# An expert layer behind polysketch attention on one core: the expert stage rewritten with 128-slot tiles

## Chip, core and metric

The kernel runs on one core of one Trainium2 chip. The metric is device time in microseconds (us) of one execution. All data is float32, except that S1 and S2 come as float64.

## What is computed

```python
def phi(x):                       # x: [batch 4, heads 4, seq 1088, 32]
    a = einsum('rd,bhsd->bhsr', S1, x); b = einsum('rd,bhsd->bhsr', S2, x)   # r = 8
    return einsum('bhsi,bhsj->bhsij', a, b).reshape(..., 64)
kv = einsum('bhsf,bhsd->bhfd', phi(k), v);  z = phi(k).sum(axis=2)
attn = (phi(q) @ kv) / (phi(q) . z + 1e-6)
x = attn as [4352 tokens, 128]
logits = x @ w_gate;  e_idx = argmax(logits)          # 8 experts, one per token
gate_w = softmax(logits)[e_idx];  eom = sigmoid(x @ w_output_gate)
out[n] = gate_w[n] * eom[n, e] * (relu(x[n] @ w1[e]) @ w2[e])    # w1: 128x1024, w2: 1024x128
```

With the inputs of the reference the eight experts get 547, 583, 461, 483, 494, 867, 420 and 497 tokens.

## The kernel before

The kernel has two stages.

**Attention and routing.** The 4352 tokens go in nine groups of up to 512. For each group `k_steps` builds the keys' features and adds up their products with the values in PSUM; `q_steps` builds the queries' features, the attention output `x` (`nd`, L310), the logits and the routing (`route`, L336 to L387). At the end of `route`, GpSimd (POOL) writes each token's row (128 values, the factor of its output and its token number) into the DRAM buffer `xs`, sorted by expert: one indirect DMA for 128 tokens (L385), 34 in all. Behind them POOL writes rows of padding behind each expert's last token (L431), so that each expert's rows fill whole tiles of `TS` slots. Meanwhile VectorE (DVE) turns the counts of tokens into two tables (L436 to L469): `eti`, the expert of each tile, and `bti`, the first row of each tile in `xs`. There is one tile for each of the `NT` steps that the program unrolls. `NT` is the most tiles that any routing could need, (4352 + 8·255) // 256 = 24; the tokens above fill 20, and the last four hold padding alone.

**Experts.** A tile is 256 slots. `fetch` (L476) lets SyncE (SP) read the tile's expert and first row from the tables into registers, and issues two DMAs: the expert's 1 MB of weights into one of three buffers (skipped where the buffer already holds this expert), and the tile's rows into `xin`. `up` (L485) turns the two 128-row halves of `xin` (two transposes on TensorE, L488), copies them to SBUF (DVE, L490) and multiplies them with w1: eight matmuls of 256 columns with the weights stationary (L495), in two PSUM tiles of four. ScalarE (ACT) takes the first tile through the relu (L497), DVE the second (L499). `down` (L502) multiplies with w2: eight matmuls with the weights stationary and the activations `hT` moving, summed in one PSUM tile (L506), whose result has the features on partitions, so that it is copied (ACT, L508), turned back by two transposes (L514), scaled by the token's factor (DVE, L517) and written to its tokens' rows of `out` by two indirect DMAs (POOL, L519). A float32 matmul appears in the trace as two MATMUL instructions, each with its own weight load (PEld), and a transpose as one.

Two things set the order of the work. Instructions are put on each engine by the scheduler of the framework, which may move them within the program's dependencies. And two writes to the same DRAM buffer are kept in order: an indirect DMA into `xs` or `out` waits until the one before it has landed.

```python
for t in range(min(NW, NT)):
    fetch(t)
up(0)
for t in range(NT):
    if t + 1 < NT:
        up(t + 1)
    yT = down(t)
    if t + NW < NT:
        fetch(t + NW)
    send(t, yT)
```

Of the kernel before, what the change touches and what calls it, by code (L numbers as in the profile page):

```python
# [29 lines left out]
def kernel(  # L30
# [61 lines left out]
    # Queries and keys with the features of two heads on partitions, twice, for the two parts of S1  # L92
    # and S2; values with tokens on partitions (two heads and a column of ones, twice).
# [47 lines left out]
    before = consts.tile([128, 128], F32, tag="before")     # [s, t]: s < t  # L141
# [16 lines left out]
    PP = 128 // E                       # partitions that pad one expert  # L158
    padsel = consts.tile([128, E], F32, tag="padsel")       # [p, e]: p // PP == e
# [18 lines left out]
    upto = consts.tile([128, E, E], F32, tag="upto")        # [e, f]: f <= e  # L178
# [4 lines left out]
    def split():  # L183
        # A float64 as two float32: the upper 23 bits of its fraction, and the lower 29.
# [88 lines left out]
    seen = {"tile": None, "at": 0}  # L273

    def q_steps(g):
# [60 lines left out]
        def route():  # L336
# [47 lines left out]
            for j in range(nj):  # L384
                nc.gpsimd.indirect_dma_start(  # L385
                    out=xs[:, :], out_offset=bass.IndirectOffsetOnAxis(ap=sloti[:, j:j + 1], axis=0),
                    in_=s["x"][:, j], in_offset=None, bounds_check=E * CAP - 1)  # L387
# [13 lines left out]
    for g in range(len(groups) + 1):  # L401
# [29 lines left out]
    nc.gpsimd.indirect_dma_start(  # L431
        out=xs[:, :], out_offset=bass.IndirectOffsetOnAxis(ap=pai[:, :1], axis=0),
        in_=pad.rearrange("p a b -> p (a b)"), in_offset=None)
# [28 lines left out]
    # A tile behind the last one falls on the padding of the last expert.  # L462
# [21 lines left out]

    def up(t):  # L485
        ps = ps_t("ps_xs")[:, :TS]
        for i in range(NI):
            nc.tensor.transpose(ps[:, i * 128:(i + 1) * 128], xin[t][:, i, :DM], ident)  # L488
# [3 lines left out]
        for g in range(FC // 4):  # L492
            ps = ps_w("ps_h").rearrange("p a (c x) -> p (a c) x", x=TS)
            for c in range(4):
                nc.tensor.matmul(ps[:, c], wt[t % NW][:, 0, 4 * g + c], xT, start=True, stop=True)  # L495
            if g % 2 == 0:
                nc.scalar.activation(hT[:, 4 * g:4 * g + 4], ps, ACTF.Relu)  # L497
            else:
                nc.vector.tensor_scalar_max(hT[:, 4 * g:4 * g + 4], ps, 0.0)  # L499
# [69 lines left out]
```

## Time and profile before

| | |
|---|---|
| time, median of three runs | 380.53 us (379.42 to 381.73) |
| span of the profiled execution | 381.2 us |
| PE busy | 302.9 us, 79% |
| weight loads (PEld) busy | 248.8 us, 65% |
| DVE, ACT, POOL busy | 117.4, 54.7, 85.2 us |
| DMA, mean over the span | 108 GB/s |
| attention and routing, last DVE step of the tables ends | 145.8 us |
| first TensorE work of the experts | 173.2 us |
| last indirect DMA issued by POOL | 372.6 us |

The profiled execution's own time is its span of 381.2 us; no time outside the span is listed for it. The page names the engines PE (matmul), PEld (weight load), DVE, ACT, POOL and SP. A line such as L495 is a line of the kernel. In rows of the timeline the columns are: start, length, engine, line, operation, out<-in with shapes, count of instructions merged into the row, and in brackets how long the engine stood idle before it and what ended that.

### The profile page before, as it was taken

Reading aid. Unit: us, or ns where it says so; the run is one execution under the profiler, and the core shown is the slowest. Engines: PE = TensorE matmul, PEld = TensorE weight load, DVE = VectorE, ACT = ScalarE, POOL = GpSimd, SP = SyncE. Lnnn points to the kernel's source line nnn. Section 1 sums busy time; section 2 is a strip of 40 time slices with the busy share of each in tenths; the row PEclk is TensorE's granted clock in tenths of the full one; section 3 lists DMA queues with packets and bytes.
Section 4 is the critical chain, followed back from the end, with each engine's and each line's share of the span. In section 5 each row is a group of like instructions: output and inputs, shape, how many; then the busy total and the mean of one; then the engine's idle time right before and its main releaser. Section 6 shows DMA issues by size and latency. Waiting matters only on the chain. (4 is left out here: it accounts for less than half of the span.)

```text
span 381.2 us, 4504 instructions
## 1 busy us (share of the span) xinstructions
PE 302.9 (79%) x1501; PEld 248.8 (65%) x1501; DVE 117.4 (31%) x413; ACT 54.7 (14%) x94; POOL 85.2 (22%) x115
## 2 busy tenths in 40 slices
PE   2979899999997530007999988999999999999950
PEld 2976677778755420006888777778778888788840
DVE  5211265635564452001222222223222232322300
ACT  1001122202221100001211111121111211112100
POOL 4000004322433333300112212322223222233231
PEclk9999899968999655556999999999999999999995
DMA  6999900000000004117345455444543544410000
GB/s 160 259 250 245 241 23 21 23 21 22 24 28 24 21 29 128 59 71 263 94 156 152 138 167 164 170 152 138 158 140 91 204 146 138 135 49 20 2 0 0
DMA packets 18870, 41.21 MB, mean 108 GB/s; under 512 B 3146, under 2 KB 9932, under 8 KB 16160
## 3 DMA queue, kind: packets, MB, share of 16 engines
q1 hardware_dynamic: 16080, 35.36, 32.4%
q0 software_dynamic: 2768, 5.57, 4.3%
q8 instruction: 12, 0.20, 0.2%
q14 instruction: 10, 0.08, 0.1%
HBM read 39.55 MB, written 6.47 MB: 121 GB/s over the span
## 5 line engine op out<-in xcount | busy, mean ns | idle before, releaser
L506 PE MATMUL ps_y<-hT,wt 128*128 128x256 f32 x384 | 90.6, 379 | 0.0
L495 PE MATMUL ps_h<-xsT,wt 128*128 128x256 f32 x384 | 89.0, 385 | 0.5 <-DVE xsT L490 0.5
L519 POOL DMA_INDIRECT out_dram<-y,xin x48 | 46.7, 972 | 166.2 <-DVE y L517 56.8
L495 PEld LDWEIGHTS ps_h<-xsT,wt 128*128 128x128 f32 x384 | 73.5, 193 | 12.4 <-DVE xsT L490 2.2
L506 PEld LDWEIGHTS ps_y<-hT,wt 128*128 128x128 f32 x384 | 71.1, 190 | 8.7
L385 POOL DMA_INDIRECT xs<-x,sloti x34 | 33.4, 983 | 119.4 <-DVE sloti L375 56.2
L499 DVE TENSOR_SCALAR hT<-ps_h 128x1024 f32<-128x1024 f32 x24 | 29.4, 1225 | 86.8 <-PE ps_h L495 69.1
L497 ACT ACTIVATE hT<-ps_h 128x1024 f32<-128x1024 f32 x24 | 24.6, 1024 | 105.6 <-PE ps_h L495 105.6
L488 PE MATMUL ps_xs<-ident,xin 128*128 128x128 f32 x48 | 9.9, 288 | 36.9 <-DMA xin<-xs 36.8
L490 DVE COPY xsT<-ps_xs 128x256 f32<-128x256 f32 x24 | 10.2, 424 | 75.9 <-PE ps_xs L488 75.9
L488 PEld LDWEIGHTS ps_xs<-ident,xin 128*128 128x128 f32 x48 | 6.1, 143 | 41.5 <-DMA xin<-xs 40.0
L265 PEld LDWEIGHTS ps_kvz<-vt,kp 128*128 128x128 f32 (+1 forms) x144 | 24.4, 255 | 8.1 <-DVE kp L244 4.1
L265 PE MATMUL ps_kvz<-vt,kp 128*128 128x65 f32 (+1 forms) x144 | 25.2, 341 | 3.8 <-DVE kp L244 3.2
L283 PE MATMUL ps_fa<-qT,Sa 128*128 128x512 f32 (+1 forms) x36 | 21.5, 714 | 1.3 <-DVE qp L295 1.3
L238 PEld LDWEIGHTS ps_ab<-S12blk,kT 128*128 128x128 f32 x136 | 20.8, 241 | 1.6 <-DVE S12blk L220 1.1
L238 PE MATMUL ps_ab<-S12blk,kT 128*128 128x32 f32 x136 | 20.9, 316 | 1.0 <-DMA kT<-in_k_dram 1.0
L508 ACT COPY yT<-ps_y 128x256 f32<-128x256 f32 x24 | 8.9, 373 | 88.5 <-PE ps_y L506 88.5
L303 PE MATMUL ps_nd<-kz,qp 128*128 128x66 f32 (+1 forms) x144 | 18.5, 279 | 1.0 <-ACT a_sb L290 1.0
L303 PEld LDWEIGHTS ps_nd<-kz,qp 128*128 128x128 f32 (+1 forms) x144 | 17.1, 191 | 3.0 <-ACT a_sb L290 1.4
L283 PE MATMUL ps_fb<-qT,Sb 128*128 128x512 f32 (+1 forms) x36 | 18.2, 633 | 0.0
L244 DVE TENSOR_TENSOR kp<-ps_ab,b_sb 128x1024 f32<-128x1024 f32 (+1 forms) x9 | 10.5, 1165 | 20.5 <-ACT b_sb L241 20.5
L295 DVE TENSOR_TENSOR qp<-a_sb,ps_fb 128x1024 f32<-128x1024 f32 (+1 forms) x9 | 10.4, 1161 | 14.8 <-PE ps_fb L283 14.8
(120 smaller groups left out, 179.1 us busy)
## 6 DMA issues: line engine op xcount, KB each, us to landing
wt<-in_w_dram SPq DMA_DIRECT2D x24, 1024.0 KB
kT<-in_k_dram SPq DMA_DIRECT2D x16, 256.0 KB, 8.5
qT<-in_q_dram SPq DMA_DIRECT2D x16, 256.0 KB, 7.8
xin<-xs SPq DMA_DIRECT2D x24, 130.0 KB, 2.2
vt<-in_v_dram SPq DMA_DIRECT2D x8, 260.0 KB, 7.2
out_dram<-y,xin POOLq DMA_INDIRECT x48, 2.3
xs<-x,sloti POOLq DMA_INDIRECT x34, 2.3
kT<-in_k_dram SPq DMA_DIRECT2D x2, 128.0 KB, 8.1
```

The costliest lines, as they stand in the source:

```text
L238: nc.tensor.matmul(ps[:, j * H + 2 * p:j * H + 2 * p + 2], kT[:, p, c * 128:(c + 1) * 128], S12blk, start=True, stop=True)
L244: nc.vector.tensor_mul(kp[:, :n], bview(av, [list(av.ap[1]), list(av.ap[2]), [0, r]]), bview(bv, [list(bv.ap[1]), [0, r], list(bv.ap[2])]))
L265: nc.tensor.matmul(acc[b][:, p], s["kp"][p0:p0 + np_, j * H + 2 * p:j * H + 2 * p + 2].rearrange("s h i j -> s (h i j)"), vt[p0:p0 + np_, ...
L283: nc.tensor.matmul(ps[:, p, :n], S_.rearrange("p h i j -> p (h i j)"), qT[:, p, cols(cs)], start=True, stop=True)
L303: nc.tensor.matmul(ps[p0:p0 + np_, p, j], s["qp"][:, p, j * 128 + p0:j * 128 + p0 + np_], kvz_done[b][:, p], start=True, stop=True)
L385: nc.gpsimd.indirect_dma_start(out=xs[:, :], out_offset=bass.IndirectOffsetOnAxis(ap=sloti[:, j:j + 1], axis=0), in_=s["x"][:, j], in_offs ...
L488: nc.tensor.transpose(ps[:, i * 128:(i + 1) * 128], xin[t][:, i, :DM], ident)
L495: nc.tensor.matmul(ps[:, c], wt[t % NW][:, 0, 4 * g + c], xT, start=True, stop=True)
L497: nc.scalar.activation(hT[:, 4 * g:4 * g + 4], ps, ACTF.Relu)
L499: nc.vector.tensor_scalar_max(hT[:, 4 * g:4 * g + 4], ps, 0.0)
L506: nc.tensor.matmul(ps, wt[t % NW][:, 1, c], hT[:, c], start=(c == 0), stop=(c == FC - 1))
L519: nc.gpsimd.indirect_dma_start(out=out, out_offset=bass.IndirectOffsetOnAxis(ap=x.bitcast(I32)[:, i, DM + 1:DM + 2], axis=0), in_=y[:, i], ...
```

## The change

The expert stage is written anew. A tile has 128 slots (`TS`), so `NT` becomes (4352 + 8·127) // 128 = 41; the tokens above fill 37. In `up` one transpose and eight matmuls of 128 columns remain, all into one two-bank PSUM tile, of which ACT takes the first half through the relu and DVE the second. In `down` the activations `hT` are the stationary side and the weights w2 the moving one: the result has tokens on partitions, so the copy and the two transposes back go away, and ACT scales by the token's factor as it empties the PSUM tile (L512 of the new file). One indirect DMA writes the tile to `out`. The indirect DMAs into `xs`, and those into `out`, are declared independent of each other (`apart`). All three weight buffers are filled with expert 0's weights right behind the loads of keys and queries, and the weight load of the first three tiles is skipped where the expert is 0. `fetch` loads the rows ahead of the weights; there are five `xin` buffers for four. SP keeps the order in which the program is written (`manual_schedule`).

```diff
-TS = 256
+TS = 128
+    def apart(group, ins):
+        tc.declare_no_dep(ins.ins, group=group, reason="the rows are distinct")
+        tc.add_to_no_dep_group(group, ins.ins)
...
+    wt = [consts.tile([128, 2, FC, 128], F32, tag=f"wt{i}", name=f"wt{i}") for i in range(NW)]
+    for i in range(NW):
+        nc.sync.dma_start(wt[i].rearrange("p a c x -> p (a c x)"), w_d[0])
...
-                nc.gpsimd.indirect_dma_start(
+                apart("rows", nc.gpsimd.indirect_dma_start(
...
     def fetch(t):
+        at = nc.sync.value_load(bti[0:1, t:t + 1], min_val=0, max_val=E * CAP - TS)
+        xin[t] = work.tile([TS, W], F32, tag="xin", bufs=NW + 2, name="xin")
+        nc.sync.dma_start(xin[t], xs[bass.ds(at, TS), :])
         regs[t] = nc.sync.value_load(eti[0:1, t:t + 1], min_val=0, max_val=E - 1)
-        kw = {} if t < NW else {"cond": regs[t] != regs[t - NW]}
         nc.sync.dma_start(wt[t % NW].rearrange("p a c x -> p (a c x)"),
-                          w_d[bass.ds(regs[t], 1)].rearrange("e p x -> p (e x)"), **kw)
-        at = nc.sync.value_load(bti[0:1, t:t + 1], min_val=0, max_val=E * CAP - TS)
...
+                          w_d[bass.ds(regs[t], 1)].rearrange("e p x -> p (e x)"),
+                          cond=regs[t] != (regs[t - NW] if t >= NW else 0))
 
     def up(t):
...
+        nc.tensor.transpose(ps, xin[t][:, :DM], ident)
...
+        ps = ps_w("ps_h").rearrange("p a (c x) -> p (a c) x", x=TS)
+        for c in range(FC):
+            nc.tensor.matmul(ps[:, c], wt[t % NW][:, 0, c], xT, start=True, stop=True)
+        nc.scalar.activation(hT[:, :FC // 2], ps[:, :FC // 2], ACTF.Relu)
+        nc.vector.tensor_scalar_max(hT[:, FC // 2:], ps[:, FC // 2:], 0.0)
...
     def down(t):
-            nc.tensor.matmul(ps, wt[t % NW][:, 1, c], hT[:, c], start=(c == 0), stop=(c == FC - 1))
-        yT = work.tile([128, TS], F32, tag="yT", name="yT")
-        nc.scalar.copy(yT, ps)
...
+        ps = psum.tile([TS, DM], F32, tag=("kvz", "rt")[t % 2], name="ps_y")
+            nc.tensor.matmul(ps, hT[:, c], wt[t % NW][:, 1, c], start=(c == 0), stop=(c == FC - 1))
+        y = work.tile([TS, DM], F32, tag="y", bufs=4, name="y")
+        nc.scalar.activation(y, ps, ACTF.Copy, scale=x[:, DM:DM + 1])
+        apart("out", nc.gpsimd.indirect_dma_start(
...
+    with tc.manual_schedule(engines={mybir.EngineType.SP}):
+        for t in range(NW):
+            fetch(t)
+        up(0)
+        for t in range(NT):
+            if t + 1 < NT:
+                up(t + 1)
+            down(t)
+            if t + NW < NT:
+                fetch(t + NW)
```

**Where the built programs put it.** The listings below give one engine's instructions in program order; a row ends with the semaphores that the instruction waits for (named after the engine or DMA lane that raises them).

TensorE in the middle of the expert stage before: `ps_h` is the first matmul of the next tile, `ps_y` the second matmul of this one, `ps_xs` and `ps_yt` the transposes.

```order
L506 MATMUL ps_y_1556<-hT_1482,wt0_1271 128x256
L495 MATMUL ps_h_1544<-xsT_1541,wt1_1272 128x256 [waits DMAHW0_49,DVE_49]
L495 MATMUL ps_h_1544<-xsT_1541,wt1_1272 128x256 x3
L495 MATMUL ps_h_1550<-xsT_1541,wt1_1272 128x256 [waits PE_49]
L495 MATMUL ps_h_1550<-xsT_1541,wt1_1272 128x256 x3
L506 MATMUL ps_y_1556<-hT_1482,wt0_1271 128x256 x7
L488 MATMUL ps_xs_1599<-ident_121,xin_1525 128x128 [waits DMAHW3_49]
```

And the same place in the changed program, one whole tile and the start of the next:

```order
L501 MATMUL ps_h_1465<-xsT_1462,wt0_121 128x128 [waits DMAHW2_49,PE_49]
L501 MATMUL ps_h_1465<-xsT_1462,wt0_121 128x128 x7
L495 MATMUL ps_xs_1511<-ident_127,xin_1448 128x128 [waits DMAHW3_49]
L510 MATMUL ps_y_1527<-wt0_121,hT_1464 128x128 [waits Activation_49]
L510 MATMUL ps_y_1527<-wt0_121,hT_1464 128x128 x3
L510 MATMUL ps_y_1527<-wt0_121,hT_1464 128x128 [waits DVE_49]
L510 MATMUL ps_y_1527<-wt0_121,hT_1464 128x128 x3
L501 MATMUL ps_h_1516<-xsT_1513,wt1_122 128x128 [waits DMAHW4_49,PE_49]
```

Before, the eight matmuls `ps_h` of the next tile stand between the first and the second `ps_y` of this one; now a tile's eight `ps_y` stand behind its own eight `ps_h` with one transpose between.

VectorE for the same tile of the changed program (`hT_1464` is written half by ACT, L502, and half by DVE, L503):

```order
L497 COPY xsT_1513<-ps_xs_1511 128x128 [waits DVE_49,PE_49]
L503 TENSOR_SCALAR hT_1464<-ps_h_1465 128x512 [waits Activation_49]
L497 COPY xsT_1564<-ps_xs_1562 128x128 [waits DVE_49,PE_49]
L503 TENSOR_SCALAR hT_1515<-ps_h_1516 128x512 [waits Activation_49]
```

and ScalarE:

```order
L512 ACTIVATE y_1485<-ps_y_1476,xin_1330 128x128 [waits DMAHW7_49,PE_49]
L502 ACTIVATE hT_1464<-ps_h_1465 128x512 [waits DVE_49,PE_49]
L512 ACTIVATE y_1536<-ps_y_1527,xin_1397 128x128 [waits DMAHW1_49,PE_49]
```

Before, each half of the relu read a PSUM tile of its own and waited for PE by itself; now both halves read one tile, and DVE's half names ACT's semaphore and no other.

SyncE at the start of the expert stage before (TENSOR_LOAD reads a table entry into a register):

```order
L477 TENSOR_LOAD eti [waits DVE_49]
L477 ISA x2
L479 ISA
L479 DMA wt_1271<-in_w_dram 128x2048 [waits DMAHW0_49]
L481 TENSOR_LOAD bti [waits DVE_49]
L481 ISA x2
L477 TENSOR_LOAD eti
```

There 42 TENSOR_LOADs stand in all between this first weight DMA and the first `xin` DMA. In the changed program:

```order
L485 TENSOR_LOAD bti [waits DVE_49]
L485 ISA x2
L487 ISA
L487 DMA xin<-xs 128x130 [waits DMAHW3_49,DMASW2_49]
L488 TENSOR_LOAD eti
L488 ISA x2
L489 REGISTER_ALU x2
L489 ISA
L489 DMA wt_121<-in_w_dram 128x2048 [waits DMAHW4_49,DMAHW0_49]
```

Now one TENSOR_LOAD stands ahead of the first `xin` DMA, and each tile's two reads stand with its two DMAs.

## Rows read from the trace of the kernel before

**Rows 1.** Windows: busy us of each engine (instructions), then PEclk, DMA share, GB/s.

```profile
300.00:350.00 50.00, 47.91 (x230) 40.74 (x229) 13.28 (x20) 8.75 (x13) 12.39 (x13) 1.00 0.36 118
```

**Rows 2.** Waits over the whole span: total us, times, longest us.

```profile
POOL xs L385 <- DMA xs<-x,sloti: 52.7, 28, 3.3
PEld ps_xs L488 <- DMA xin<-xs: 40.0, 10, 32.4
```

**Rows 3.** Timeline, 140 to 175 us: from the routing to the experts.

```profile
142.31 0.16 DVE L381 TENSOR_TENSOR x<-co,ex 128x2 f32<-128x2 f32 x1
...
143.68 0.17 DVE L461 CAST eti<-et 128x24 int32<-128x24 f32 x1
...
144.02 0.35 DVE L464 TENSOR_TENSOR tu<-tu,num 128x192 f32<-128x192 f32 x1
...
144.89 0.37 SPq L479 DMA_DIRECT2D wt<-in_w_dram  x1
...
145.58 0.18 DVE L469 CAST bti<-bt 128x24 int32<-128x24 f32 x1
...
156.58 0.97 POOL L385 DMA_INDIRECT xs<-x,sloti  x1 [1.64 <-DMA xs<-x,sloti]
159.70 0.96 POOL L431 DMA_INDIRECT xs<-pad,pai  x1 [2.15 <-DMA xs<-x,sloti]
170.93 0.41 SPq L483 DMA_DIRECT2D xin<-xs  x1
...
173.17 0.69 PE L488 MATMUL ps_xs<-ident,xin 128*128 128x128 f32 x2 [32.35 <-DMA xin<-xs]
...
174.37 5.27 PE L495 MATMUL ps_h<-xsT,wt 128*128 128x256 f32 x16 [0.52 <-DVE xsT L490]
```

**Rows 4.** DMA issues: count and median us from issue to landing.

```profile
xs<-x,sloti POOLq DMA_INDIRECT x34, 2.3
...
xs<-pad,pai POOLq DMA_INDIRECT x1, 4.9
```

**Rows 5.** Timeline, 298 to 318 us: a weight load, and one tile of the experts.

```profile
300.41 0.35 SPq L479 DMA_DIRECT2D wt<-in_w_dram  x1
...
301.61 3.62 PE L495 MATMUL ps_h<-xsT,wt 128*128 128x256 f32 x16
...
305.06 3.19 PE L506 MATMUL ps_y<-hT,wt 128*128 128x256 f32 x14
...
308.33 0.37 ACT L508 COPY yT<-ps_y 128x256 f32<-128x256 f32 x1 [3.73 <-PE ps_y L506]
...
308.76 0.44 PE L514 MATMUL ps_yt<-ident,yT 128*128 128x128 f32 x2 [0.30 <-ACT yT L508]
...
309.47 3.62 PE L495 MATMUL ps_h<-xsT,wt 128*128 128x256 f32 x16
```

**Rows 6.** Timeline of PE, 60 to 100 us: matmuls of few columns.

```profile
70.70 1.87 PE L238 MATMUL ps_ab<-S12blk,kT 128*128 128x32 f32 x16
72.41 1.04 PE L323 MATMUL ps_l<-wg,xT 128*128 128x16 f32 x8
```

**Rows 7.** Timeline, 100 to 141 us: ACT and DVE over 512 columns of PSUM.

```profile
120.61 0.59 ACT L320 COPY xT<-ps_xt 128x512 f32<-128x512 f32 x1 [2.53 <-PE ps_xt L318]
...
121.55 0.69 DVE L295 TENSOR_TENSOR qp<-a_sb,ps_fb 128x512 f32<-128x512 f32 x1 [0.91 <-PE ps_fb L283]
```

**Rows 8.** Windows of 1 us: PE busy (instructions), PEclk, DMA share, GB/s.

```profile
117.00:118.00 1.00, 0.10 (x1) 1.00 0.00 0
...
177.00:178.00 1.00, 1.00 (x5) 0.73 0.99 418
...
304.00:305.00 1.00, 1.00 (x6) 1.00 0.96 349
305.00:306.00 1.00, 1.00 (x7) 1.00 0.27 80
```

**Rows 9.** Timeline, 352 to 382 us: the end.

```profile
367.80 0.37 ACT L508 COPY yT<-ps_y 128x256 f32<-128x256 f32 x1 [4.04 <-PE ps_y L506]
...
372.59 0.97 POOL L519 DMA_INDIRECT out_dram<-y,xin  x1 [1.43 <-DMA out_dram<-y,xin]
```

More of the change, by code (lines that the diff above doesn't have):

```diff
@@ L384, in route @@
             for j in range(nj):
-                nc.gpsimd.indirect_dma_start(
+                apart("rows", nc.gpsimd.indirect_dma_start(
                     out=xs[:, :], out_offset=bass.IndirectOffsetOnAxis(ap=sloti[:, j:j + 1], axis=0),
-                    in_=s["x"][:, j], in_offset=None, bounds_check=E * CAP - 1)
+                    in_=s["x"][:, j], in_offset=None, bounds_check=E * CAP - 1))
         return fa, fb, nd, logits, route
@@ L430 @@
     nc.vector.tensor_copy(pai, pa)
-    nc.gpsimd.indirect_dma_start(
+    apart("rows", nc.gpsimd.indirect_dma_start(
         out=xs[:, :], out_offset=bass.IndirectOffsetOnAxis(ap=pai[:, :1], axis=0),
-        in_=pad.rearrange("p a b -> p (a b)"), in_offset=None)
+        in_=pad.rearrange("p a b -> p (a b)"), in_offset=None))
     tk = consts.tile([128, E, KN], F32, tag="tk")
@@ L469 @@
     nc.vector.tensor_copy(bti, bt)
-    wt = [consts.tile([128, 2, FC, 128], F32, tag=f"wt{i}", name=f"wt{i}") for i in range(NW)]
-    NI = TS // 128
     regs, xin, hTs = {}, {}, {}
     def fetch(t):
+        at = nc.sync.value_load(bti[0:1, t:t + 1], min_val=0, max_val=E * CAP - TS)
+        xin[t] = work.tile([TS, W], F32, tag="xin", bufs=NW + 2, name="xin")
+        nc.sync.dma_start(xin[t], xs[bass.ds(at, TS), :])
         regs[t] = nc.sync.value_load(eti[0:1, t:t + 1], min_val=0, max_val=E - 1)
-        kw = {} if t < NW else {"cond": regs[t] != regs[t - NW]}
         nc.sync.dma_start(wt[t % NW].rearrange("p a c x -> p (a c x)"),
-                          w_d[bass.ds(regs[t], 1)].rearrange("e p x -> p (e x)"), **kw)
-        at = nc.sync.value_load(bti[0:1, t:t + 1], min_val=0, max_val=E * CAP - TS)
-        xin[t] = work.tile([128, NI, W], F32, tag="xin", bufs=NW + 1, name="xin")
-        nc.sync.dma_start(xin[t], xs[bass.ds(at, TS), :].rearrange("(i p) w -> p i w", p=128))
+                          w_d[bass.ds(regs[t], 1)].rearrange("e p x -> p (e x)"),
+                          cond=regs[t] != (regs[t - NW] if t >= NW else 0))
     def up(t):
         ps = ps_t("ps_xs")[:, :TS]
-        for i in range(NI):
-            nc.tensor.transpose(ps[:, i * 128:(i + 1) * 128], xin[t][:, i, :DM], ident)
+        nc.tensor.transpose(ps, xin[t][:, :DM], ident)
         xT = work.tile([128, TS], F32, tag="xsT", name="xsT")
@@ L491, in up @@
         hT = work.tile([128, FC, TS], F32, tag="hT", name="hT")
[L492 to L499, printed above, removed]
+        ps = ps_w("ps_h").rearrange("p a (c x) -> p (a c) x", x=TS)
@@ L500, in up @@
+        for c in range(FC):
+            nc.tensor.matmul(ps[:, c], wt[t % NW][:, 0, c], xT, start=True, stop=True)
+        nc.scalar.activation(hT[:, :FC // 2], ps[:, :FC // 2], ACTF.Relu)
+        nc.vector.tensor_scalar_max(hT[:, FC // 2:], ps[:, FC // 2:], 0.0)
         hTs[t] = hT
     def down(t):
-        hT = hTs.pop(t)
-        ps = psum.tile([128, TS], F32, tag="kvz", name="ps_y")
+        hT, x = hTs.pop(t), xin.pop(t)
+        ps = psum.tile([TS, DM], F32, tag=("kvz", "rt")[t % 2], name="ps_y")
@@ L505, in down @@
         for c in range(FC):
-            nc.tensor.matmul(ps, wt[t % NW][:, 1, c], hT[:, c], start=(c == 0), stop=(c == FC - 1))
-        yT = work.tile([128, TS], F32, tag="yT", name="yT")
-        nc.scalar.copy(yT, ps)
-        return yT
-    def send(t, yT):
-        ps = psum.tile([128, NI, DM], F32, tag="rt", name="ps_yt")
-        for i in range(NI):
-            nc.tensor.transpose(ps[:, i], yT[:, i * 128:(i + 1) * 128], ident)
-        y = work.tile([128, NI, DM], F32, tag="y", bufs=3, name="y")
-        x = xin.pop(t)
-        nc.vector.tensor_tensor(y, ps, x[:, :, DM:DM + 1].to_broadcast((128, NI, DM)), op=ALU.mult)
-        for i in range(NI):
-            nc.gpsimd.indirect_dma_start(
-                out=out, out_offset=bass.IndirectOffsetOnAxis(ap=x.bitcast(I32)[:, i, DM + 1:DM + 2], axis=0),
-                in_=y[:, i], in_offset=None, bounds_check=N - 1, oob_is_err=False)
@@ L523 @@
-    for t in range(min(NW, NT)):
-        fetch(t)
-    up(0)
-    for t in range(NT):
-        if t + 1 < NT:
-            up(t + 1)
-        yT = down(t)
-        if t + NW < NT:
-            fetch(t + NW)
-        send(t, yT)
+            nc.tensor.matmul(ps, hT[:, c], wt[t % NW][:, 1, c], start=(c == 0), stop=(c == FC - 1))
+        y = work.tile([TS, DM], F32, tag="y", bufs=4, name="y")
+        nc.scalar.activation(y, ps, ACTF.Copy, scale=x[:, DM:DM + 1])
+        apart("out", nc.gpsimd.indirect_dma_start(
+            out=out, out_offset=bass.IndirectOffsetOnAxis(ap=x.bitcast(I32)[:, DM + 1:DM + 2], axis=0),
+            in_=y, in_offset=None, bounds_check=N - 1, oob_is_err=False))
```

## Prediction

> **What bounds the kernel now.** I read the windows first, then the waits, then the timeline at the places that they point to. The reader is to see two different limits.
>
> In the expert stage TensorE is the limit. In 300 to 350 us it is busy for 47.91 of 50 us at a granted clock of 1.00, with the DMA engines at 0.36 [rows 1]. One tile is the stretch from one run of 16 `ps_h` instructions to the next, 309.47 - 301.61 = 7.86 us [rows 5]. The run itself goes from 301.61 to 305.06, so an instruction of 256 columns takes 3.45/16 = 0.2157 us. The 32 of a tile make 6.90 us, and transposes and one wait for ACT the other 0.96.
>
> Between the stages the limit is a queue. TensorE waits up to 32.4 us for the first `xin` [rows 2]. The timeline shows three things ahead of it [rows 3]. (a) POOL's scatters go one at a time: it waits 28 times, 52.7 us in all, for its previous scatter to land [rows 2]. So although the last values of `x` are there at 142.47, the last scatter starts at 156.58 and the padding at 159.70. The padding takes 4.9 us to land [rows 4], so it is there at 164.6. (b) The table `bti` is ready at 145.76. (c) SP issues the first weights at 144.89, but the first `xin` only at 170.93, 6.3 us after the padding landed. The built program shows 42 register reads between the two; 26.04/42 = 0.62 us each. So (c) ends the wait, and (a) alone would leave it at 164.6. The first transpose follows 2.24 us behind `xin`, at 173.17.
>
> **The sum, part by part.** The base is the profiled span, 381.2 us; the median of the runs, 380.53, is 0.7 less, which I leave out. A measurement of this kernel can tell about 0.5% from no change, some 2 us.
>
> *The start.* Two edits act here, and only both together reach it. Unordered scatters: POOL's last two can start once `x` is ready at 142.47 [rows 3]; each holds POOL for 0.97, so the padding starts at 144.4. It has half the bytes. Its landing lies between the 2.3 us of a plain scatter and the old 4.9 [rows 4]; I take the middle, 3.6, so it is there at 148.0. Earlier scatters, and the waits behind them on POOL, end under the attention work. SP in program order: one register read stands ahead of the first `xin`. From `eti` ready (143.85) to the weight DMA behind it 1.04 us went by [rows 3]; I take that. The tables grow from 24 to 41 tiles: about ten chained DVE steps of up to 0.35 us [rows 3] grow by between nothing and 41/24, or 0 to 2.5 us; I take 1.5, since a part of each step does not grow. So `bti` is ready at 147.3, `xin` is issued at 148.3 (the padding has just landed) and the first transpose starts at 150.5. From there to the first `ps_h` 1.20 us went by [rows 3]; with one transpose for two, 0.95. The experts start at 151.45 instead of 174.37: **-22.9 us**.
>
> *The pace.* A matmul instruction now has 128 columns, and 32 of them make a tile. Its cost is not in the trace. From above: 0.2157, if halving the columns saved nothing. From below: the weight load that goes with every instruction. Sixteen instructions of 32 columns take 72.41 - 70.70 = 1.71 us, 0.107 each [rows 6], so the load sets their pace. At 256 columns this load is hidden completely (0.2157 a piece, load included). Half of 0.2157 is 0.108, next to the lower end, so I take 0.11: 3.52 us a tile.
>
> *A new wait, inside each tile.* Before, the next tile's `ps_h` run stood between a tile's relu and most of its `ps_y`. Now `ps_y` follows its own `ps_h`, with only a transpose between. DVE's relu names ACT's semaphore and not PE's, so ACT's half must already have waited for the eighth matmul. The chain is: last `ps_h` instruction to ACT 0.25 (308.33 less 305.06 + 14 x 0.2157) [rows 5]; ACT over 512 columns 0.59 [rows 7]; ACT to the weight load 0.06 (308.70 to 308.76) [rows 5]; the load of `hT` ahead of the first matmul, which nothing covers, 0.107. That is 1.0 us per tile, the transpose (0.11) lying inside. DVE's half starts 0.9 us after the last `ps_h` and takes 0.69 [rows 7], to 1.63 with its hand-over; the fifth `ps_y` matmul loads at 0.9 + 8 x 0.11 = 1.78. It is covered by 0.15; each 0.1 us beyond that would cost 41 x 0.1 = 4 us.
>
> A tile then takes 3.52 + 1.0 = 4.52 us, 0.59 of the old one, but 41 run for 24. From 151.45: the first `ps_h` run 1.76, then 40 tiles 180.8, then 1.0 + 1.76 gives 336.8. At the start of the stage TensorE stood at half its clock until about 177.5, some 4.3 us behind the first transpose [rows 3, 8]; 3.5 us of matmuls there cost 1.7 more, so the last `ps_y` ends at 338.5. The stage lasts 187.05, against 193.2 (174.37 to 367.55, 0.25 ahead of the last ACT copy [rows 9]): **-6.1 us**. So the copy and transposes saved, and fewer padded slots, nearly all go into the new wait.
>
> *Loads.* The three early weight loads run behind those of keys and queries and before any expert: nothing. By the inputs' routing 21 later tiles load weights. A load may start when `ps_y` of tile t ends and is needed by `ps_h` of t+3, two tiles or 9 us later. Issued at 300.41, it had the DMA engines busy into 305 to 306 [rows 5, 8], about 5 us: hidden, with 4 to spare. Should it be late, 21 loads late by 1.6 us each would eat the whole gain. SP's two reads and two issues per tile, some 2 us, are hidden in 4.5 as well. DVE and ACT have 1 us of work each per tile.
>
> *The end.* Before, the last ACT copy began at 367.80, two scatters followed in order, the last at 372.59, and the span ended 8.6 us later [rows 9]. Now ACT (0.25 after the last matmul, 0.25 long) is followed by one scatter, which I put 0.7 behind it: 338.5 + 1.2 + 8.6 = 348.3, 9.8 behind the last matmul against 13.65: **-3.85 us**.
>
> Sum: 381.2 - 22.9 - 6.1 - 3.85 = 348.3, said as **348 us**.
>
> [...] In the trace weight loads hide under matmuls of the same size: 16 instructions of 256 columns each bring a 128x128 load and still take 0.2157 apiece [rows 5], though a load alone paces at 0.107 [rows 6]. [...]
>
> **The rivals.**
> - *Loads no longer hidden* (slower). At 128 columns load and matmul are equally long, and any friction between them shows. Price: 41 x 32 = 1312 instructions, 1.3 us per ns. It decides from 0.11 + 33/1312 = 0.135 us an instruction; in full series, 0.217, the time is 348 + 140 = 488. For it: no row shows two equal ones. Against: both rows at hand show full overlap [rows 5, 6]. Chance 0.04.
> - *The clock falls* (slower). The new gap leaves TensorE idle for about 0.9 of 4.5 us, 41 times. The stage holds 41 x 3.52 = 144 us of matmuls; if half of them ran at the half clock, the time would be 348 + 72 = 420, and it turns slower than before from 33/144 = 23%. For it: the clock was low after the long wait [rows 8]. Against: with PE busy for 0.10 of 117 to 118 us it still read 1.00 [rows 8]. Chance 0.06.
> - *No gap* (faster). If ACT can start on the first four matmuls, a tile is 33 x 0.11 = 3.63 us, 0.89 less, and the time 348 - 36 = 312. Against it stands the semaphore that DVE lacks. Chance 0.04.
> - *The start does not move*, because something behind the scatters and reads holds `xin` (the padding, or the larger tables): 348 + 22.7 = 371, so the "ahead" part would have done nothing. Against: the order shows the reads moved and the scatters free. Chance 0.04.
>
> **How the numbers follow.** The forecast has 0.82. Its range: down by 4 with instructions of 0.107, by 6 with a gap of 0.85, by 1 with an earlier `xin`: 337. Up by 13 with 0.12 an instruction, by 4 with a gap of 1.1, by 1 with the padding at 4.9 us: 366. The four rivals lie outside, 0.18 together. Faster by over 0.5%: the forecast, no gap, an unmoved start and a mild form of the first two rivals, 0.91; slower 0.07; within 0.5% 0.02.
>
> **What would show it.** Right: first expert transpose near 150.5; the `xin` DMA the only thing TensorE waits for there; runs of 16 instructions of 128 columns in about 1.75 us, one tile every 4.5 us; ACT's relu 0.25 behind the last `ps_h`; TensorE's idle time named "ACT hT" and about 0.9 us a tile; granted clock 1.00. Wrong: a pace far from 0.11, a clock below 1 in the stage, `ps_y` waiting for DVE, or `ps_h` waiting for `wt`.

## The result and the profile after

| | before | after |
|---|---|---|
| time, median (range) | 380.55 us (379.42 to 381.73) | 341.13 us (338.96 to 343.47) |
| span of the profiled execution | 381.2 us | 337.2 us |
| first expert transpose, first `ps_h` | 173.17, 174.37 us | 139.71, 140.57 us |
| last matmul (0.25 ahead of the last ACT copy) | 367.55 us | 328.19 us |

The changed kernel takes 0.894 of the time of the one before (95% interval 0.887 to 0.901). The forecast was 348, with a range of 337 to 366. Ratios here and below leave out executions that fell into the chip's slower state; medians and ranges hold all. The profiled execution of the changed kernel took 338.96 us at a span of 337.2: times of this kernel lie some 1.7 us above their spans, and this one lies 2.2 us below the median. Later executions of the kernel before took 1.8 to 2.1 us more than their spans, so its profile, with a span of 381.2, belongs to an execution some 2.6 us above its median.

Between the two profiled executions the span fell by 44.0 us: 33.8 in the start (up to the first `ps_h`), 5.6 in the stage (193.2 to 187.6) and 4.6 at the end (13.65 to 9.0). The medians fell by 39.4 us; most of the other 4.6 is due to which executions were profiled.

From the page after: busy time, and the granted clock in 40 slices of 8.4 us.

```profile
PE 275.0 (82%) x1990; PEld 243.4 (72%) x1990; DVE 106.9 (32%) x423; ACT 60.4 (18%) x128; POOL 77.2 (23%) x108
...
PEclk9999999999999975589999999999999999999997
```

Waits of the changed kernel (total us, times, longest us), to be read against [rows 2]:

```profile
PEld ps_y L510 <- ACT hT L502: 33.5, 41, 0.9
...
PE ps_y L510 <- ACT hT L502: 23.7, 41, 0.7
...
PE ps_xs L495 <- DMA xin<-xs: 11.7, 1, 11.7
```

POOL's 52.7 us of waiting for its own scatters are gone. TensorE waits once for rows, 11.7 us where it was 32.4, and in each of the 41 tiles it now waits for ACT's relu.

The start, from the timeline of the changed kernel (against [rows 3]):

```profile
129.98 0.16 DVE L391 TENSOR_TENSOR x<-co,ex 128x2 f32<-128x2 f32 x1
...
134.22 0.96 POOL L441 DMA_INDIRECT xs<-pad,pai  x1 [0.30 <-issue]
136.61 0.19 DVE L479 CAST bti<-bt 128x41 int32<-128x41 f32 x1
137.90 0.36 SPq L487 DMA_DIRECT2D xin<-xs  x1
...
139.71 0.48 PE L495 MATMUL ps_xs<-ident,xin 128*128 128x128 f32 x1 [11.68 <-DMA xin<-xs]
...
140.57 3.78 PE L501 MATMUL ps_h<-xsT,wt 128*128 128x128 f32 x16 [0.38 <-DVE xsT L497]
```

The last values of `x` are there 12.3 us earlier than before (130.14 for 142.47). The padding follows 4.1 us later and `xin` 3.7 us behind it. `bti` is ready 1.1 us ahead of `xin`, and of the two SyncE's waits name it alone. The padding's landing is not in this profile; in the 3.6 us that it takes in e11_noout it would land at 137.8, so table and padding end this wait almost together.

One tile, from the same timeline:

```profile
237.73 1.95 PE L501 MATMUL ps_h<-xsT,wt 128*128 128x128 f32 x16
...
239.52 0.27 PE L495 MATMUL ps_xs<-ident,xin 128*128 128x128 f32 x1
239.72 0.60 ACT L502 ACTIVATE hT<-ps_h 128x512 f32<-128x512 f32 x1 [1.42 <-PE ps_h L501]
...
240.35 0.69 DVE L503 TENSOR_SCALAR hT<-ps_h 128x512 f32<-128x512 f32 x1 [0.23 <-ACT hT L502]
...
240.37 2.05 PE L510 MATMUL ps_y<-wt,hT 128*128 128x128 f32 x16 [0.58 <-ACT hT L502]
...
242.26 0.94 PE L501 MATMUL ps_h<-xsT,wt 128*128 128x128 f32 x7
```

A tile takes 242.26 - 237.73 = 4.53 us. ACT begins only when all eight `ps_h` matmuls are done, and DVE behind ACT, as the semaphores in the order said. The last row has fewer instructions than 16 only because the stretch was cut there.

### The profile page after: what moved, and what is told of

Read it like the earlier page. It is cut to its first block, busy times and chain, and to the rows that moved or that the text cites. A ratio compares the mean times of both kernels' runs of the same rounds, so it can differ in the third digit from the quotient of the medians.

```text
span 337.2 us, 5768 instructions
## 1 busy us (share of the span) xinstructions
PE 275.0 (82%) x1990; PEld 243.4 (72%) x1990; DVE 106.9 (32%) x423; ACT 60.4 (18%) x128; POOL 77.2 (23%) x108
## 4 chain that ended last, share of the span: by engine, by line
issue 45%; PE 30%; POOL 12%; DVE 5%; DMA 3%; POOLq 1%; ACT 1%; SPq 1%; ACTq 0%
POOL out_dram L513 11%; PE ps_kvz L275 6%; PE ps_ab L248 6%; PE ps_nd L313 5%; PE ps_fa L293 4%; PE ps_fb L293 4%; PE ps_l L333 2%; DVE kp L254 1%; DMA kT<-in_k_dram 1%; PE ps_xt L328 1%; DMA xs<-pad,pai 1%; PE ps_pos L367 1%; POOLq L513 1%; PE ps_pos L368 1%; DMA xin<-xs 1%
## 5 line engine op out<-in xcount | busy, mean ns | idle before, releaser
L510 PE MATMUL ps_y<-wt,hT 128*128 128x128 f32 x656 | 84.4, 282 | 23.7 <-ACT hT L502 23.7
L510 PEld LDWEIGHTS ps_y<-wt,hT 128*128 128x128 f32 x656 | 76.6, 192 | 33.5 <-ACT hT L502 33.5
L501 PE MATMUL ps_h<-xsT,wt 128*128 128x128 f32 x656 | 81.8, 279 | 0.4 <-DVE xsT L497 0.4
L501 PEld LDWEIGHTS ps_h<-xsT,wt 128*128 128x128 f32 x656 | 78.2, 195 | 0.7 <-DVE xsT L497 0.7
L513 POOL DMA_INDIRECT out_dram<-y,xin x41 | 39.8, 970 | 155.1 <-ACT y L512 155.1
L497 DVE COPY xsT<-ps_xs 128x128 f32<-128x128 f32 x41 | 11.9, 291 | 137.1 <-PE ps_xs L495 133.8
L502 ACT ACTIVATE hT<-ps_h 128x512 f32<-128x512 f32 x41 | 24.5, 597 | 73.3 <-PE ps_h L501 73.3
L503 DVE TENSOR_SCALAR hT<-ps_h 128x512 f32<-128x512 f32 x41 | 28.3, 691 | 12.9 <-ACT hT L502 12.8
L512 ACT ACTIVATE y<-ps_y,xin 128x128 f32<-128x128 f32 x41 | 15.1, 367 | 88.1 <-PE ps_y L510 88.1
L495 PE MATMUL ps_xs<-ident,xin 128*128 128x128 f32 x41 | 11.5, 281 | 11.7 <-DMA xin<-xs 11.7
L293 PE MATMUL ps_fa<-qT,Sa 128*128 128x512 f32 (+1 forms) x36 | 19.1, 644 | 0.0
L305 DVE TENSOR_TENSOR qp<-a_sb,ps_fb 128x1024 f32<-128x1024 f32 (+1 forms) x9 | 10.4, 1160 | 12.6 <-PE ps_fb L293 12.0
```

The lines of the kernel that those rows point to most:

```text
L293: nc.tensor.matmul(ps[:, p, :n], S_.rearrange("p h i j -> p (h i j)"), qT[:, p, cols(cs)], start=True, stop=True)
L495: nc.tensor.transpose(ps, xin[t][:, :DM], ident)
L501: nc.tensor.matmul(ps[:, c], wt[t % NW][:, 0, c], xT, start=True, stop=True)
L502: nc.scalar.activation(hT[:, :FC // 2], ps[:, :FC // 2], ACTF.Relu)
L503: nc.vector.tensor_scalar_max(hT[:, FC // 2:], ps[:, FC // 2:], 0.0)
L510: nc.tensor.matmul(ps, hT[:, c], wt[t % NW][:, 1, c], start=(c == 0), stop=(c == FC - 1))
```

## The experiments

All kernels compute everything. "Pitch" is the mean from the second `ps_h` run to the last, over 39 tiles: for the changed kernel (323.71 - 147.23) / 39 = 4.53 us. The times of before were 378.81 us beside the first four runs, 382.17 beside the next four and 379.28 beside the last four; ratios are to the before of the same four.

| kernel | first `ps_h` | pitch | time, median | ratio to before (95%) |
|---|---|---|---|---|
| changed kernel | 140.57 | 4.53 | 341.13 | 0.894 (0.887 to 0.901) |
| e1_rows | 143.96 | | 354.14 | 0.937 (0.926 to 0.947) |
| e2_start | 144.01 | | 352.93 | 0.937 (0.927 to 0.946) |
| e3_sp | 165.57 | | 375.59 | 0.993 (0.989 to 0.997) |
| e4_stage | 173.38 | 4.21 | 361.43 | 0.956 (0.944 to 0.968) |
| e5_norows | 163.25 | 4.53 | 361.98 | 0.949 (0.941 to 0.958) |
| e6_split | 144.48 | 3.79 | 312.86 | 0.819, from the medians (308.90 to 313.61 us, for 378.60 to 384.36) |
| e7_ahead | 146.38 | 4.57 | 345.36 | 0.903 (0.894 to 0.913) |
| e8_ahead4 | 148.12 | 3.72 | 312.60 | 0.813 (0.804 to 0.822) |
| e9_nosp | 138.78 | | 339.55 | 0.898 (0.892 to 0.904) |
| e10_nopre | 144.21 | | 345.25 | 0.911 (0.907 to 0.916) |
| e11_noout | 140.92 | | 339.22 | 0.897 (0.891 to 0.904) |
| e12_aheadx | 142.66 | 4.39 | 338.46 | 0.896 (0.888 to 0.905) |

### The start: which of its two edits moved it

**e1_rows**: the kernel before, with the scatters into `xs` and the padding declared independent, and nothing else.

```diff
-                nc.gpsimd.indirect_dma_start(
+                apart("rows", nc.gpsimd.indirect_dma_start(
...
-    nc.gpsimd.indirect_dma_start(
+    apart("rows", nc.gpsimd.indirect_dma_start(
```

> The kernel before with one edit: the scatters into xs (and the padding) are declared independent. In the built program this also changes two orders: TensorE's work of the last three groups of the attention stands in the order of the changed kernel, and 3 register reads instead of 42 stand ahead of the first xin on SyncE. Theory: the start moves because nothing waits for scatters or reads any more, and the attention's end comes 8 us earlier by the new order (and up to 5 us more where the clock does not dip in it): first expert transpose at 139 to 146, time 347 to 354. Rival (the attention's gain is due to the early weights or the clock alone, not to the order): first transpose at 150 or later, time 357 to 360.

Measured: 354.14 us, -24.7 against its before. From its timeline:

```profile
131.66 0.37 SPq L483 DMA_DIRECT2D wt<-in_w_dram  x1
...
133.47 0.96 POOL L435 DMA_INDIRECT xs<-pad,pai  x1 [0.30 <-issue]
140.44 0.41 SPq L487 DMA_DIRECT2D xin<-xs  x1
...
142.75 0.69 PE L492 MATMUL ps_xs<-ident,xin 128*128 128x128 f32 x2 [15.42 <-DMA xin<-xs]
```

This one edit moves the first expert transpose from 173.17 to 142.75. The 42 register reads no longer hold it: with the ordering gone the scheduler put three reads ahead of the first `xin`. What holds `xin` now is the padding, which in this kernel takes 7.0 us to land. The first weight load, 1 MB, was issued 1.8 us ahead of it, and the DMA engines were busy throughout from 134 to 138 us:

```profile
134.00:138.00 4.00, 0.00 (x0) 0.00 (x0) 0.00 (x0) 0.00 (x0) 0.43 (x1) 0.50 1.00 369
```

**e2_start**: e1_rows, and SyncE in program order (the edit of e3_sp).

> The kernel before with independent scatters and SyncE in program order. Theory: with 3 reads ahead of the first xin there is little left for SyncE's order to give: within 2 us of the kernel with independent scatters alone. Rival: the order of SyncE is worth the 6 us by which its reads came later than the padding, so 6 us faster than that kernel.

Measured: 352.93 us, transpose at 142.80. Behind free scatters the manual order of SyncE adds nothing that can be seen.

**e3_sp**: the kernel before with SyncE in program order alone.

```diff
-    for t in range(min(NW, NT)):
-        fetch(t)
+    with tc.manual_schedule(engines={mybir.EngineType.SP}):
+        for t in range(min(NW, NT)):
+            fetch(t)
```

> The kernel before with SyncE in program order alone. Theory: the first xin is then released by the padding, which landed at 164.6 in the trace of before, so the first transpose moves from 173.2 to 167 and the time by 6, to 374. Rival (the reads only stood beside the wait): no change, 380.

Measured: 375.59 us, -3.2, about half of what was expected. The timeline shows `xin` released by the padding, 4.83 us behind its issue, as the theory said:

```profile
157.26 0.96 POOL L431 DMA_INDIRECT xs<-pad,pai  x1 [2.13 <-DMA xs<-x,sloti]
162.09 0.41 SPq L483 DMA_DIRECT2D xin<-xs  x1
```

**e5_norows**: the changed kernel with the scatters into `xs` and the padding in order again (the diff of e1_rows turned round).

> The changed kernel with the scatters into xs in order again. Theory (the declaration of independence is worth what the kernel before gained by it, through the chain of scatters and the order of the attention's tail): the padding goes out at 157 to 160 and lands 3.3 us later, first expert transpose at 162 to 166 instead of 140, time 360 to 365. Rival (the early weights and SyncE's order carry the start by themselves): below 350.

Measured: 361.98 us, as the theory said, with the first transpose at 162.39. POOL waits for its scatters again and SyncE for the padding:

```profile
POOL xs L395 <- DMA xs<-x,sloti: 51.1, 28, 3.4
...
SPq L487 <- DMA xs<-pad,pai: 13.7, 1, 13.7
```

Taken away, the declaration costs the changed kernel 0.949 - 0.894 = 5.5% of the time before, some 21 us; put in alone it gave 6.3%. It is the largest part of the change.

**e9_nosp**: the changed kernel without the manual order of SyncE.

```diff
-    with tc.manual_schedule(engines={mybir.EngineType.SP}):
-        for t in range(NW):
-            fetch(t)
+    for t in range(NW):
+        fetch(t)
```

> The changed kernel with SyncE left to the scheduler. Its program then has six register reads ahead of the first xin where the changed kernel has one; behind them each tile's reads stand with its two DMAs nearly as before. Theory (the manual order is worth nothing once the scatters are free): five of the six reads are of eti, which is ready 2.9 us before bti, and five reads take about 3.1 us; so xin goes out 0 to 1 us later and the time is 340 to 343 us. Rival (the order is what keeps rows and weights in time): a wait for wt or xin appears in the stage, at 0.5 us or more in each of the 21 tiles that load, and the time is 351 us or more.

Measured: 339.55 us, no slower than the changed kernel; no wait for `wt` or `xin` appears in the stage. No gain from the manual order can be seen here.

**e10_nopre**: the changed kernel without the three early weight loads.

```diff
-    for i in range(NW):
-        nc.sync.dma_start(wt[i].rearrange("p a c x -> p (a c x)"), w_d[0])
```

> The changed kernel without the three early weight loads. Theory: the first ps_h waits for weights that are issued behind the first xin, as it did for 3.94 us in e4_stage, less what the transpose and its copy cover anyway; the second and third tile's loads hide behind the 4.5 us of a tile. Time 343.5 to 346 us, 3 to 4 us above the changed kernel. Rival 1 (the three loads queue up, each about 4 us, and the second and third tile wait as well): 348 us or more. Rival 2 (the loads hide behind the scatters' landing): 341 us.

Measured: 345.25 us, 4.1 above the changed kernel's median, which was taken beside other executions of before; by the ratios, 0.911 against 0.894, it is 1.7% of the time before, some 6 us. The profiles show 3.6 us of it at the start: the first `ps_h` waits for its weights, once:

```profile
144.21 3.73 PE L499 MATMUL ps_h<-xsT,wt 128*128 128x128 f32 x16 [3.95 <-DMA wt<-in_w_dram]
```

So the early loads do earn their place, though only behind a first `xin` that comes at 138: in the kernel before the weights were there long ahead of the rows.

### The stage: the wait inside a tile

**e4_stage**: the new stage alone; the changed kernel without the free scatters into `xs`, the early weights and the order of SyncE (the diffs of e5_norows, e10_nopre and e9_nosp together).

> The changed kernel's expert stage alone: ordered scatters into xs, no early weights, SyncE left to the scheduler (44 reads stand ahead of the first xin). Theory: the start is as late as before (first xin near 172, and the first weights behind it, so that the first ps_h is near 178), the stage lasts 187 to 188 us and the end 9 us: time 372 to 377, a gain of 4 to 9. Rival (the stage as such is the source of the gain): below 365.

Measured: 361.43 us, over 10 us faster than expected. That is below the 365 of the rival, so the stage alone did give a gain in this program. The start moved by 1 us only (first `ps_h` at 173.38, behind 3.94 us of waiting for weights), but the stage was shorter: its last matmul ends at 348.1, 174.7 us later, against 187.6 in the changed kernel. Its timeline, one tile:

```profile
249.75 0.60 ACT L500 ACTIVATE hT<-ps_h 128x512 f32<-128x512 f32 x1 [3.04 <-PE ps_h L499]
...
250.40 1.38 PE L508 MATMUL ps_y<-wt,hT 128*128 128x128 f32 x10
251.62 1.99 PE L499 MATMUL ps_h<-xsT,wt 128*128 128x128 f32 x16
253.45 0.83 PE L508 MATMUL ps_y<-wt,hT 128*128 128x128 f32 x6
253.65 0.60 ACT L500 ACTIVATE hT<-ps_h 128x512 f32<-128x512 f32 x1 [3.04 <-PE ps_h L499]
```

Here the scheduler set the next tile's 16 `ps_h` instructions between the first ten `ps_y` instructions of a tile and its last six; in other tiles it split them twelve to four or fourteen to two. The relu then has work beside it. In the last 14 tiles the order is that of the changed kernel again, and so is the wait:

```profile
341.73 2.05 PE L508 MATMUL ps_y<-wt,hT 128*128 128x128 f32 x16 [0.58 <-ACT hT L500]
343.62 1.95 PE L499 MATMUL ps_h<-xsT,wt 128*128 128x128 f32 x16
```

The pitch is 4.03 us on average over the 25 tiles before and 4.53 over these 14, which makes the 4.21 of the table. So the wait for ACT does not come from the size of the tile; it comes with the order on TensorE, which the scheduler chose otherwise here. Which of the three edits cost the changed kernel this order stays open: with any one of them taken out (e5_norows, e9_nosp, e10_nopre) nearly every tile still takes 4.53 us.

**e6_split**: the changed kernel with each half of `ps_h` in a PSUM tile of its own, so that ACT can start on the first half.

```diff
-        ps = ps_w("ps_h").rearrange("p a (c x) -> p (a c) x", x=TS)
+        for g in range(2):
+            ps = ps_w("ps_h")[:, 0].rearrange("p (c x) -> p c x", x=TS)
...
+            if g == 0:
+                nc.scalar.activation(hT[:, own], ps, ACTF.Relu)
+            else:
+                nc.vector.tensor_scalar_max(hT[:, own], ps, 0.0)
```

> The changed kernel, but each half of the relu reads a PSUM tile of its own, so that ACT can start behind the fourth of the eight ps_h matmuls; the order of TensorE is the same. Theory (the idle 0.9 us of each tile is ACT's wait for the eighth matmul and its 0.59 us): the first ps_y follows the transpose at once, the fifth waits about 0.1 us for DVE's half, one tile takes 3.7 to 3.8 us instead of 4.53, time 306 to 312. Rival (TensorE needs the time anyway, by loads or by DVE): above 330.

Measured: 312.86 us, 28 below the changed kernel and a little above the theory's 306 to 312. One tile of its timeline:

```profile
221.85 1.95 PE L503 MATMUL ps_h<-xsT,wt 128*128 128x128 f32 x16
...
222.99 0.60 ACT L505 ACTIVATE hT<-ps_h 128x512 f32<-128x512 f32 x1 [0.57 <-PE ps_h L503]
...
223.74 2.06 PE L514 MATMUL ps_y<-wt,hT 128*128 128x128 f32 x16
223.89 0.69 DVE L507 TENSOR_SCALAR hT<-ps_h 128x512 f32<-128x512 f32 x1 [2.90 <-ACT hT L505]
...
225.63 1.95 PE L503 MATMUL ps_h<-xsT,wt 128*128 128x128 f32 x16
```

ACT starts 1.14 us into the `ps_h` run and ends before the run does, so `ps_y` follows without a wait; a tile takes 225.63 - 221.85 = 3.78 us. With the order of TensorE as it was, this takes 0.75 us off a tile: they came from two engines reading one PSUM tile that was released as a whole. Together with e4_stage it shows that the wait needs both, the shared tile and `ps_y` right behind its own `ps_h`.

**e7_ahead** and **e8_ahead4** leave that tile whole and put TensorE's work in a written order instead: transposes two tiles ahead, `ps_h` one tile ahead of `ps_y`. e7_ahead has three weight buffers; e8_ahead4 differs by `NW = 4`, which also makes six `xin` buffers of five.

```diff
+    with tc.manual_schedule(engines={mybir.EngineType.SP, mybir.EngineType.PE}):
...
+            if t + 2 < NT:
+                turn(t + 2)
             if t + 1 < NT:
                 up(t + 1)
             down(t)
```

> The changed kernel with TensorE in a written order: the transpose of tile t+2, ps_h of tile t+1, then ps_y of tile t; the relu reads one PSUM tile as before. Theory: the relu has a whole tile of time, so a tile takes 33 x 0.109 = 3.6 us; but a weight load may only start behind ps_y of t and is needed 3.7 us later by ps_h of t+3, against 5 us for the load, so about two of three loads of each expert are waited for by 1.3 us: time 318 to 326, and TensorE's waits name wt. Rival (loads are not late): 304 to 308.

> The same with four weight buffers (and all four filled ahead, six xin buffers). Theory: the load has 7.3 us, no wait for wt is left, one tile takes 3.6 us: time 303 to 308. Rival (the DMA engines are the limit, with up to four loads per expert): as with three buffers or above.

Measured: 345.36 and 312.60 us, the first some 20 us above what was expected, the second some 5. In e7_ahead the wait for ACT is gone and, where the theory had named `wt`, a wait for rows has come:

```profile
PE ps_xs L497 <- DMA xin<-xs: 39.4, 17, 12.6
```

e8_ahead4 lost all but some 3 us of it (beside the start's 12.6), and TensorE is busy throughout (160 to 240 us; columns as in [rows 1]):

```profile
160.00:240.00 80.00, 79.21 (x711) 79.02 (x710) 20.64 (x42) 20.62 (x43) 21.38 (x22) 1.00 0.88 297
```

Its pitch is 3.72 us. The time equals that of e6_split because in this run the stage began 3.6 us later.

**e12_aheadx**: e7_ahead with each tile's rows fetched one tile earlier, ahead of the weight load that they stood behind. It asks what e7_ahead really lacked, early rows or a fourth weight buffer.

```diff
+            if t + NW + 1 < NT:
+                rows(t + NW + 1)
             if t + NW < NT:
                 fetch(t + NW)
```

> The kernel of e7_ahead (PE one tile ahead, three weight buffers) with each tile's rows fetched one tile earlier, ahead of the weight load behind which they stood, and six xin buffers. Theory (three weight buffers leave a load too little time in this order: it can start when ps_y of tile t ends and is needed by ps_h of t+3, one tile of 3.7 us later, while a load takes about 5 us; xin only landed behind it): the waits move from xin to wt, some 1 to 2 us in each of about 20 tiles, and the time stays at 335 to 347 us. Rival (the late rows alone made e7_ahead slow): no such wait is left, a tile takes 3.69 us as in e8_ahead4, and the time is 309 to 318 us.

Measured: 338.46 us. The wait for rows is gone, and a wait for weights stands in its place:

```profile
PE ps_h L509 <- DMA wt<-in_w_dram: 21.7, 16, 2.6
```

So the wait that e7_ahead's profile names was mostly not the cause. The rows landed behind weights that were late as well, and freeing the rows gave 0.18 us of the 0.85 a tile between e7_ahead (4.57) and e8_ahead4 (3.72). The rest belongs to the weights, since the fourth weight buffer is all that e8_ahead4 has beyond the six `xin` buffers of this kernel: in this order a load has one tile of 3.7 us to arrive where the changed kernel gives it two of 4.5. Part of the difference is the clock: from 160 to 240 us it was granted at 0.98 in e12_aheadx and at 1.00 in e8_ahead4, which is an estimated 0.02 x 4.39 = 0.09 us a tile.

**e11_noout**: the changed kernel with the 41 scatters into `out` in order.

```diff
-        apart("out", nc.gpsimd.indirect_dma_start(
+        nc.gpsimd.indirect_dma_start(
```

> The changed kernel with the 41 scatters into out in order. Theory: a scatter comes every 4.5 us and one holds POOL for 0.97 and lands some 2.3 us behind its issue, so the one before has landed when it is asked for; 340 to 343 us, POOL's waits all on ACT's y. Rival (a scatter of 128 rows into out lands later than 3.5 us, so each waits for the one before and the y buffers fill up): the pace of a tile goes from 4.5 to 5 us or more, and the time is 361 us or more.

Measured: 339.22 us, no change. DMA issues, count and median us to landing:

```profile
out_dram<-y,xin POOLq DMA_INDIRECT x41, 3.5
...
xs<-pad,pai POOLq DMA_INDIRECT x1, 3.6
```

A scatter lands in 3.5 us and the next comes 4.5 us later, so order costs nothing at this pace.

## Why the prediction was right, and 7 us too high

**The pace of a matmul: right.** An instruction of 128 columns was put at 0.11. The 16 `ps_y` of the tile above run from 240.37 to 242.15, when the next load begins: 1.78/16 = 0.111.

**The new wait: right.** The tile was put at 4.52 and takes 4.53; the whole stage at 187.05 and takes 187.6. ACT's relu starts 0.21 behind the end of the `ps_h` run (237.73 + 16 x 0.111 = 239.51), `ps_y` 0.86 behind it. DVE covers its half, and TensorE's idle time is named "ACT hT" 41 times. The rival "no gap" was rightly set aside for this program, but its price, 312, is what e6_split measured once the shared PSUM tile was cut.

**Loads in the stage and the clock: right.** TensorE never waits for `wt` after the change. The granted clock was 0.50 at 141 to 143 us, behind the 11.68 us of waiting, and 1.00 at 250 to 300 us: the first run of 16 `ps_h` took 3.78 us, the later ones 1.95. The windows:

```profile
141.00:142.00 1.00, 1.00 (x6) 1.00 (x6) 0.00 (x0) 0.00 (x0) 0.00 (x0) 0.50 0.26 67
142.00:143.00 1.00, 1.00 (x7) 1.00 (x6) 0.00 (x0) 0.00 (x0) 0.00 (x0) 0.50 0.02 8
...
250.00:300.00 50.00, 43.65 (x368) 41.04 (x367) 10.89 (x23) 10.61 (x22) 10.67 (x11) 1.00 0.47 155
```

**The end: right.** 9.8 us behind the last matmul were forecast, 9.0 came: POOL issues at 329.07, 0.63 behind ACT's start, and the span ends 8.1 later.

**The start: the step that failed.** It was to give -22.9 and gave -33.8. The sentence at fault is "POOL's last two can start once `x` is ready at 142.47". It kept the time of `x` from the old trace, as if free scatters changed nothing ahead of them. The terms:

| from | to | forecast | after |
|---|---|---|---|
| start | last values of `x` | 142.47 | 130.14 |
| `x` | padding issued | 1.9 | 4.1 |
| padding issued | `xin` issued | 3.9 | 3.7 |
| `xin` | first transpose | 2.2 | 1.8 |
| transpose | `ps_h` | 0.95 | 0.86 |

The 12.3 us at `x` have two main sources. The first is TensorE's clock in the attention. The window of 78 to 86 us of the kernel before (columns as in [rows 1]):

```profile
78.00:86.00 8.00, 8.00 (x32) 5.76 (x31) 2.43 (x10) 0.13 (x1) 2.81 (x3) 0.57 0.05 17
```

The same window of the changed kernel:

```profile
78.00:86.00 8.00, 8.00 (x55) 6.45 (x55) 4.43 (x14) 1.06 (x3) 3.88 (x4) 1.00 0.08 26
```

TensorE is busy throughout in both, and was granted 0.57 in the first and 1.00 in the second. This makes 4.9 us by the transposes of `x` that start at 106.73 before and at 101.86 after. It is no part of the change: e3_sp, whose attention is that of the kernel before with its scatters in order, was granted 1.00 all through 60 to 100 us, and its transposes start at 101.29. Such slices stand at different places in the profiles here (why, no run shows), and the profile of before lies 2.6 us above its median. In e1_rows, for one, the granted clock falls in the fifth to seventh slice:

```profile
PEclk9999888999999855599999999999999999999995
```

Another 7.9 us arise behind these transposes, since `ps_n`, the last matmul of the routing, starts at 140.22 before and at 127.43 after (12.8 less 4.9; from there to `x` 0.5 is lost again). TensorE's timeline of the kernel before, at the last groups:

```profile
112.72 1.93 PE L283 MATMUL ps_fb<-qT,Sb 128*128 128x512 f32 x4
115.96 1.13 PE L283 MATMUL ps_fa<-qT,Sa 128*128 128x256 f32 x4 [1.31 <-DVE qp L295]
118.13 2.00 PE L303 MATMUL ps_nd<-kz,qp 128*128 128x66 f32 x16 [1.04 <-ACT a_sb L290]
119.97 0.60 PE L318 MATMUL ps_xt<-ident,x 128*128 128x128 f32 x4
```

And of the changed kernel, at the same groups:

```profile
107.80 1.94 PE L293 MATMUL ps_fb<-qT,Sb 128*128 128x512 f32 x4
111.08 0.66 PE L328 MATMUL ps_xt<-ident,x 128*128 128x128 f32 x4 [1.34 <-DVE x L320]
111.57 1.03 PE L293 MATMUL ps_fa<-qT,Sa 128*128 128x256 f32 x4
112.76 1.06 PE L333 MATMUL ps_l<-wg,xT 128*128 128x16 f32 x8 [0.16 <-ACT xT L330]
113.68 1.98 PE L313 MATMUL ps_nd<-kz,qp 128*128 128x66 f32 x16
```

Before, the transposes that lead to the routing stand behind the next group's `ps_fa` and `ps_nd`, each of which waits; after, they come first. The code of the attention is the same. The runs show which edit does it: the step that takes `ps_n` out of PSUM starts at 137.6, 137.0 and 139.2 us in e3_sp, e4_stage and e5_norows, whose scatters are ordered, and at 127.4, 127.6, 125.3 and 127.7 in e1_rows, e2_start, e9_nosp and e11_noout, whose scatters are free. The profiles' clocks do not make this difference: from the same transposes to `ps_n` it is 33.5, 35.7, 33.1 and 33.3 us in before, e3_sp, e4_stage and e5_norows, and 25.6, 24.0, 23.9, 23.9 and 24.2 in the changed kernel, e1_rows, e2_start, e9_nosp and e11_noout. How much of it is the order itself, and how much the granted clock of that stretch (0.50 at 130 to 140 us before), is not separated. The built programs held this difference in order, and the prediction read their order for the expert stage alone.

Smaller terms ran against it. The scatters run back to back, 1.28 us apart, and had fallen behind: when `x` was ready three were still to go, where the prediction had counted two and nothing ahead of them. And the sum of 348.3 is a span but was read as a time. Against the span of 337.2 it is 11.1 us too high; the 1.7 us from span to time, and the 2.2 by which the profiled execution lies below the median, bring this down to 7. So part of the closeness is luck.

**"Only both together reach it": wrong.** e1_rows reached it with one edit, since the same declaration that frees POOL lets the scheduler place the reads elsewhere. With ordered scatters the order of SyncE is worth 3.2 us, behind free ones nothing (e2_start, e9_nosp).

**The early weights: no cost, as forecast, but also some 4 us that the sum owes to them** (e10_nopre). The sum let the first `ps_h` follow the first transpose and did not say that, with the rows fetched ahead of the weights, the early weights are what allows this.

## What to carry to other kernels

Declaring DMAs independent does more than let them overlap: it takes edges out of the graph from which the scheduler orders every engine, so the queue of the waiting engine must be read again in the built program, the stages ahead of it included. Where two engines share the emptying of one PSUM tile and TensorE has nothing else to do meanwhile, give each its own: that was worth 28 us here, where the smaller tiles and the transposes saved had given 5.6 in the stage. A wait names what landed last; before paying for an earlier transfer, ask whether what it stood behind is late too (e7_ahead, e12_aheadx).

## What the runs showed that was not expected

- **Weight loads stay hidden where load and matmul are equally long.** In the tile above 16 loads and 16 matmuls of 128 columns take 0.111 us a pair, where instructions of 32 columns, throughout which PEld is busy (1.70 of 1.70 us from 70.7 to 72.4 before), pace at 0.107 [rows 6]. If load and matmul ran one after the other, they would make a tile an estimated 32 x 0.107 = 3.4 us longer than the 4.53 us that the trace shows.
- **The padding lands later beside a weight load.** With 256 slots it takes 4.9 us (before) and 4.8 (e3_sp) where the first weight load was issued some 15 us earlier, and 7.0 and 6.8 (e1_rows, e2_start) where it was issued 1.8 us earlier. With 128 slots and no weight load beside it, it takes 3.6 behind free scatters (e11_noout), and `xin` follows its issue by 3.7 us behind ordered ones (e5_norows) and without early weights (e10_nopre) alike. So the scatters make no difference that can be seen; halving the padding is worth some 1.2 us, and keeping the weight load away from it some 2. That the load is the cause was not tested by itself.
- **The tables grew by 1.4 us as estimated, but not in this execution.** From `num` to `bti` it is 4.7 us in e1_rows and 6.1 to 6.2 in e4_stage, e5_norows and e6_split, but 8.5 in the changed kernel's profile, with 1.24 us of idle time at one step. Why stays open. It cost next to nothing: `xin` follows the padding by 3.7 us here as in e5_norows and e10_nopre, where the table was ready 4 us or more ahead of `xin`.
